# Sigmoid attention, then an MLP mixer: the first two batches mixed singly, and all work written in the order of a model of readiness

One Trainium2 chip (trn2), one core. The metric is the device time of one execution in microseconds (us), lower is better; the output has to agree with the reference.

## The reference

Eight batches, 12 heads, 448 positions, head size 64. Attention with a sigmoid in place of softmax makes x; a mixer with two layers over tokens and two over channels follows.

```python
scores = np.matmul(q, k.transpose(0, 1, 3, 2)) / np.sqrt(64) - np.log(448)
x = np.matmul(1.0 / (1.0 + np.exp(-scores)), v)      # (8, 12, 448, 64)
x = x.transpose(0, 2, 1, 3).reshape(8, 448, 768)
h = np.maximum(x.transpose(0, 2, 1) @ w_tok1, 0.0) @ w_tok2      # 448 -> 256 -> 448
u = x + h.transpose(0, 2, 1)
out = u + np.maximum(u @ w_ch1, 0.0) @ w_ch2                    # 768 -> 1536 -> 768
```

## The kernel before

The batches are taken in four pairs; the two batches of a pair lie on the two halves of the 128 partitions. While TensorE mixes the channels of pair g, the attention of pair g+1 is woven in between. The channel products use Strassen's scheme: seven products in place of eight, paid for by sums of rows of u (the "s" and "r" tiles), sums of weights, and VectorE copies ("c") of partial results. Each engine has a queue of its own and takes it in the order in which the program wrote the instructions, so the written order is part of the design.

The copy that puts one pair of heads into the layout that the transposing DMA takes, on VectorE:

```python
    def permute(g, i, what):
        m = pa.tile([128, J, 2, E], FP16, tag=f"p{what}", bufs=1, name=f"p{what}_{g}_{i}")
        nc.vector.tensor_copy(
            out=m[:, :, :, :], in_=raws[(g, i, what)].rearrange("p h j e -> p j h e")
        )
```

The sums of rows, all on VectorE, and the relu of product 4 of channel layer one, there too:

```python
    def row_sums(a11, a12, a21, a22, s2, s3, s4):
        def one(o, x, y, op):
            return lambda: nc.vector.tensor_tensor(out=o, in0=x, in1=y, op=op)
    # ... (four sums)
            elif p == 4:
                mm(bk[(cb, "x")], 4, cb, False)
                nc.vector.tensor_scalar(
                    out=h[:, cb, :, 1, :],
                    in0=bk[(cb, "x")].rearrange("c (j p) -> c j p", j=J),
                    scalar1=0.0,
                    scalar2=None,
                    op0=MAX,
                )
```

The order: fixed positions, and the attention spread by a cost per piece.

```python
    def weave(mix, side, att, upto):
        each = sum(c for c, _ in mix[:upto]) / (len(att) + 1)
        # ... (before each channel product: as many attention steps as are due)
            f()
            at += c
            # ...
            run(side.get(m, []))
    # ... (for each pair g: sums at fixed places in the list of channel products)
            after(1, lambda g=g: ch1_sums(g, 0, J)[3]())
            # ...
                for j0, j1, ats in (
                    (0, 4, (b1 + 11, b1 + 11, b1 + 12)),
                    (4, 6, (b1 + 14, b1 + 14, b1 + 14)),
                    (6, 7, (b1 + 15, b1 + 15, b1 + 15)),
                ):
```

## Time and profile before

| | before |
|---|---|
| median of the 3 runs made before the change | 437.9 us (433.66 to 438.22) |
| span of the profiled execution | 439.5 us, granted clock 0.957 |
| TensorE busy | 372.5 us, 85% |
| up to the first channel product | 79.4 us |
| the three stages with attention beside the mixing | 95.2, 99.7, 98.6 us |
| last pair's mixing, layer one and layer two | 29.6 and 25.5 us |
| tail without products | 11.6 us |

Stages are cut in TensorE's timeline at the first channel product of each unit. A "gap" is the idle time in brackets that the timeline prints with the first instruction after it, with what released it. A "granted clock" under 1.00 means that the array ran part of the stretch at half clock.

### The profile page before, as it was taken

Reading aid. Unit: us, or ns where it says so; the run is one execution under the profiler, and the core shown is the slowest. Engines: PE = TensorE matmul, PEld = TensorE weight load, DVE = VectorE, ACT = ScalarE, POOL = GpSimd, SP = SyncE. Lnnn points to the kernel's source line nnn. Section 1 sums busy time; section 2 is a strip of 40 time slices with the busy share of each in tenths; the row PEclk is TensorE's granted clock in tenths of the full one; section 3 lists DMA queues with packets and bytes.
Section 4 is the critical chain, followed back from the end, with each engine's and each line's share of the span. In section 5 each row is a group of like instructions: output and inputs, shape, how many; then the busy total and the mean of one; then the engine's idle time right before and its main releaser. Section 6 shows DMA issues by size and latency. Waiting matters only on the chain.

```text
span 439.5 us, 8012 instructions
## 1 busy us (share of the span) xinstructions
PE 372.5 (85%) x3204; PEld 178.6 (41%) x3204; DVE 289.0 (66%) x547; ACT 196.3 (45%) x231; POOL 122.4 (28%) x227
## 2 busy tenths in 40 slices
PE   2888778799799899869979899769999899899990
PEld 1444333344344444324434444324444444344550
DVE  2467656987885488646754578746673578898760
ACT  1897546666366233637656133545776133000000
POOL 8780403033333112243234211332310111000130
PEclk9999969999899999969989999988999999999996
DMA  8999899367556449686677539776670239200232
GB/s 105 192 164 201 120 172 124 50 104 109 84 78 104 102 85 167 119 110 108 98 101 115 108 68 141 148 114 94 104 104 1 73 72 154 81 1 0 72 103 78
DMA packets 74581, 45.39 MB, mean 103 GB/s; under 512 B 51632, under 2 KB 71856, under 8 KB 74544
## 3 DMA queue, kind: packets, MB, share of 16 engines
q0 software_dynamic: 26192, 32.94, 44.4%
q1 hardware_dynamic: 48352, 11.93, 17.4%
q8 instruction: 25, 0.41, 0.4%
q14 instruction: 12, 0.10, 0.1%
HBM read 43.84 MB, written 11.01 MB: 125 GB/s over the span
## 4 chain that ended last, share of the span: by engine, by line
PE 53%; DVE 19%; DMA 11%; ACT 8%; issue 5%; POOL 2%; POOLq 0%; DVEq 0%; ACTq 0%; SPq 0%
PE x L563 8%; PE x L438 7%; PE qk L212 6%; PE xa L228 6%; DMA q<-in_q_dram 6%; ACT attn L219 5%; PE k L295 5%; PE z L563 4%; DVE c L453 4%; PE z L438 4%; PE yn L318 4%; PE d L610 3%; DMA uT<-u 3%; DVE h2T L456 3%; PE xb L255 2%
## 5 line engine op out<-in xcount | busy, mean ns | idle before, releaser
L219 ACT ACTIVATE attn<-qk 128x896 f16<-128x896 f32 x168 | 145.7, 917 | 76.0 <-PE qk L212 69.6
L438 PEld LDWEIGHTS <-w 128*128 128x128 f16 x504 | 46.0, 100 | 78.5 <-issue 47.3
L512 POOL DMA_DIRECT2D out_dram<-u x56 | 29.4, 531 | 149.1 <-DVE u L574 147.1
L212 PE MATMUL qk<-qT,kT 64*64 64x448 f16 x672 | 62.0, 395 | 9.0 <-ACT attn L219 4.9
L453 DVE COPY c<-x 128x448 f32<-128x448 f32 x72 | 44.6, 619 | 15.2 <-PE x L438 13.4
L438 PE MATMUL x<-s,w 128*128 128x448 f16 x144 | 37.2, 369 | 10.4 <-DVE c L453 10.4
L438 PE MATMUL x<-uT,w 128*128 128x448 f16 x144 | 37.4, 371 | 7.8 <-DVE h2T L456 6.0
L228 PE MATMUL xa<-attn,v 64*64 64x448 f16 x672 | 41.3, 366 | 0.0
L202 POOL COPY gate<-qT 1x2 f16<-1x2 f16 x16 | 2.8, 175 | 128.8 <-DMA qT<-pq 128.8
L212 PEld LDWEIGHTS <-kT 64*64 64x64 f16 x672 | 19.5, 109 | 45.5 <-issue 41.3
L574 DVE TENSOR_TENSOR u<-u,x 128x384 f32<-128x384 f32 x48 | 26.5, 551 | 16.5 <-PE x L563 16.0
L107 POOL DMA_DIRECT2D k<-in_k_dram x48 | 29.1, 616 | 25.8 <-DVE pk L161 16.0
L563 PEld LDWEIGHTS <-h2T 128*128 128x128 f16 x288 | 26.3, 98 | 22.4 <-issue 6.8
L327 DVE TENSOR_TENSOR u<-x_nat,yn 128x384 f32<-128x384 f16 x56 | 28.9, 549 | 7.0 <-PE yn L318 6.8
L456 DVE CUSTOM_DVE_ANT_0 h2T<-z,c 128x448 f16<-128x448 f32 x48 | 29.8, 621 | 4.7 <-PE z L438 3.9
L245 ACT ACTIVATE xT<-xa 128x896 f16<-128x896 f32 x18 | 16.5, 917 | 30.6 <-PE xa L228 30.6
L107 POOL DMA_DIRECT2D q<-in_q_dram x48 | 29.2, 626 | 2.4 <-DVE c L453 2.1
L107 POOL DMA_DIRECT2D v<-in_v_dram x48 | 29.4, 638 | 1.0 <-DMA w_tok_t<-in_moe_w_tok_dram 0.6
L346 ACT ACTIVATE u<-u 128x768 f16<-128x768 f32 x21 | 17.7, 843 | 24.6 <-DVE u L327 18.9
L563 PE MATMUL x<-w,r 128*128 128x384 f16 x144 | 27.5, 327 | 0.8 <-DVE u L574 0.8
L574 DVE TENSOR_TENSOR u<-u,z 128x384 f32<-128x384 f32 x24 | 13.2, 552 | 22.5 <-PE z L563 22.3
L318 PE MATMUL yn<-h1T,w_tok_n 128*64 128x384 f16 x224 | 25.4, 339 | 3.1 <-DVE kT L176 1.3
(58 smaller groups left out, 467.2 us busy)
## 6 DMA issues: line engine op xcount, KB each, us to landing
out_dram<-u POOLq DMA_DIRECT2D x56, 192.0 KB, 3.3
k<-in_k_dram POOLq DMA_DIRECT2D x48, 112.0 KB, 2.9
q<-in_q_dram POOLq DMA_DIRECT2D x48, 112.0 KB, 4.1
v<-in_v_dram POOLq DMA_DIRECT2D x48, 112.0 KB, 4.4
w<-in_moe_w_ch_dram POOLq DMA_DIRECT2D x2, 2304.0 KB, 17.6
w_tok_t<-in_moe_w_tok_dram POOLq DMA_DIRECT2D x2, 224.0 KB, 5.8
uT<-u SPq DMA_TRANSPOSE x21, 4.4
kT<-pk SPq DMA_TRANSPOSE x17, 3.3
```

The source lines that it names most:

```text
L107: nc.gpsimd.dma_start(out=t[64 * b : 64 * b + 64, :, :, :], in_=src[2 * g + b, 2 * i : 2 * i + 2].rearrange("h (p j) e -> p h j e", j=J),)
L212: nc.tensor.matmul(out=ps[64 * b : 64 * b + 64, h, 0:S], lhsT=kT[(g, i)][r, j, b, :], rhs=qT[(g, i)][r, :, b, :], start=True, stop=True,)
L219: nc.scalar.activation(out=at[:, :, :], in_=ps[:, :, 0:S], func=SIGMOID, bias=att_bias, scale=att_scale)
L228: nc.tensor.matmul(out=ps[b][64 * h : 64 * h + 64, :], lhsT=vf[r, h, j, :], rhs=attn[(g, i, j)][r, h, :], start=(j == 0), stop=(j == J - 1),)
L318: nc.tensor.matmul(out=ps[64 * b : 64 * b + 64, :], lhsT=w_tok2_n[:, tcb, j, :], rhs=h1T[(g, half, tcb)][:, b, :], start=(tcb == 0), stop= ...
L327: nc.vector.tensor_tensor(out=u_of(g, j)[:, DH * half : DH * half + DH], in0=x_of(g, half)[:, j, :], in1=ps[:, :], op=ADD,)
L438: nc.tensor.matmul(out=ps[:, :], lhsT=W(p, n, cb), rhs=A[p](n), start=(first and n == 0), skip_group_check=True, stop=(n == KD - 1),)
L453: nc.vector.tensor_copy(out=s[:, :], in_=bk[(cb, "x")][:, :])
L456: nc.vector._custom_dve(dve_ops.TENSOR_ADD_SAT, out=h[:, KC * half + cb, :, b, :], in0=ps.rearrange("c (j p) -> c j p", j=J), in1=snap[(cb ...
L512: nc.gpsimd.dma_start(out=out[2 * g + b].rearrange("(p j) d -> p j d", j=J)[:, j, :], in_=us[(g, j)][64 * b : 64 * b + 64, :],)
L563: nc.tensor.matmul(out=ps[:, :], lhsT=A(p, n, kb), rhs=W(p, kb), start=(first and kb == 0), skip_group_check=True, stop=(kb == KC - 1),)
L574: nc.vector.tensor_tensor(out=u, in0=u, in1=ps[:, :], op=ADD)
```

## The change

Its intent: start the channel products sooner by mixing the first two batches (A and B) one at a time, with the two head halves of a single batch on the two partition sides; multiply these directly, without sums or copies; move the rearranging copies and some sums to GpSimd and one relu to ScalarE; and write everything in an order that a small model of costs and readiness gives while the program is built.

```diff
+    UNITS = ["A", "B", 1, 2, 3]
+    SIDES = {
+        "A": ((0, 0), (0, 6)),
+        "B": ((1, 0), (1, 6)),
+        **{g: ((2 * g, 0), (2 * g + 1, 0)) for g in (1, 2, 3)},
+    }
+    BY_DVE = ("A", "B", 1)
+    RELU4 = "act"
+    BANK = 0.4
@@ the copies @@
-        nc.vector.tensor_copy(
+        nc.gpsimd.tensor_copy(
             out=m[:, :, :, :], in_=raws[(g, i, what)].rearrange("p h j e -> p j h e")
         )
+        did("pool", 0.95, [("raw", g, i, what)], [("linear", g, i, what)], 0.1)
@@ the sums of layer two's rows, called r @@
+                nc.gpsimd if n and g < 3 else nc.vector, KC * 128, ("R", g, n), [("h", g)], ...
@@ direct products of a single batch; 72 matmuls here, 168 in layer two @@
+            for n in range(NDB):
+                ...
+                nc.tensor.matmul(
+                    out=ps[:, :],
+                    lhsT=w1[:, n, 128 * cb : 128 * cb + 128],
+                    rhs=uTs[g][:, n % KD, :, n // KD, :],
@@ A's and B's token layer two: fixed banks 2 and 3 of the four @@
+                ops.append(lambda: uturn_single(g, j - 2, 3))
+                ops.append(lambda: tok2_single(g, j, 2))
@@ the model: when is an input there, when is an engine free @@
+    def did(engine, cost, needs, gives, tail=0.0):
+        t = max([clock[engine]] + [there.get(key, 0.0) for key in needs])
+        clock[engine] = t + cost
+        for key in gives:
+            there[key] = t + cost + tail
+        return t
@@ a sum of rows is written when it would be ready for an idle VectorE, or at its last position @@
+                    soon = t_of(keys) <= clock["pe"] and clock["dve"] <= clock["pe"] + 0.2
+                    if soon or pos >= last:
@@ the sums of layer one's rows: last position 1000 products later, that is, none @@
+                    side.append(
+                        (first, first + 1000, keys, lambda g=g, j0=j0, j1=j1, m=m: ch1_sums(g, j0, j1)[m][1]())
+                    )
```

(Cuts: the loads' order, the transposes of the first seven pairs, the lists that `merge` goes through, the rest of `merge`.) The copies of x and the token relu of A, B and pair 1 also go from ScalarE to VectorE (`BY_DVE`).

## The prediction

> **What bounds the kernel now.** I read the page's busy shares first, then the stretches, then single gaps in the timeline and the chain of waits.
>
> ```profile
> PE 372.5 (85%) x3204; PEld 178.6 (41%) x3204; DVE 289.0 (66%) x547; ACT 196.3 (45%) x231; POOL 122.4 (28%) x227
> PE   2888778799799899869979899769999899899990
> ...
> PEclk9999969999899999969989999988999999999996
> ```
>
> TensorE is the busiest engine and works in every slice but the first and the last; no other engine is near full over the span. So the time is TensorE's own work plus its gaps. Where those are, the busy times by stretch show (columns: stretch, length, busy time of PE, PEld, DVE, ACT, POOL with counts, granted clock, DMA share, GB/s):
>
> ```profile
> 0.00:79.40 79.40, 57.81 (x663) 29.02 (x664) 45.44 (x86) 50.10 (x61) 36.90 (x66) 0.94 1.00 153
> 79.40:174.10 94.70, 85.28 (x734) 40.21 (x733) 72.48 (x144) 45.05 (x53) 24.70 (x47) 0.98 0.59 95
> 174.10:273.50 99.40, 89.70 (x767) 41.36 (x766) 62.49 (x116) 50.56 (x59) 28.34 (x54) 0.95 0.69 110
> 273.50:372.90 99.40, 88.85 (x768) 41.26 (x768) 64.02 (x121) 50.63 (x59) 23.78 (x46) 0.97 0.58 96
> 372.90:402.00 29.10, 25.74 (x126) 12.12 (x125) 25.16 (x46) 0.00 (x0) 1.40 (x3) 1.00 0.11 35
> 402.00:428.00 26.00, 25.08 (x153) 14.66 (x150) 18.82 (x37) 0.00 (x0) 6.06 (x12) 1.00 0.25 69
> 428.00:439.50 11.50, 0.00 (x0) 0.00 (x0) 0.54 (x1) 0.00 (x0) 1.25 (x3) 0.71 0.28 86
> ```
>
> Rows: the prologue (attention of batches 0 and 1, no channel product before 79.4 us); three stages, each mixing one pair of batches while the next pair's attention runs beside it; the last pair's mixing in its two layers; the tail, in which only the last stores land. From start-to-start times in TensorE's timeline, a stage of undisturbed work is: 42 score steps of 0.24 us, 10.1; six value products of 1.35, 8.1; six turnings of x of 0.48, 2.9; token products 4 x 1.24 and 7 x 0.77, 10.4; channel layer one, 42 pieces of 0.57, 23.9; layer two, 25 pieces of 0.975, 24.4; about 5 for some fifty changes between whole-array and quarter-array products at 0.1 each. Sum 84.8 us, against 99.4 twice. The missing 14.5 us have a pattern, here in the stage that begins at 174 (TensorE's timeline):
>
> ```profile
> 187.09 0.57 PE L212 MATMUL qk<-qT,kT 64*64 64x448 f16 x8
> 190.68 1.28 PE L438 MATMUL x<-uT,w 128*128 128x448 f16 x3 [3.02 <-DVE h2T L456]
> ...
> 198.66 0.73 PE L438 MATMUL z<-uT,w 128*128 128x448 f16 x3
> ```
>
> And the chain of waits over the same time:
>
> ```profile
> 185.97 3.43 DMA q<-in_q_dram
> 189.40 0.04 DVEq L161
> 189.43 0.04 issue
> 189.48 0.62 DVE pq L161
> 190.10 0.54 DVE h2T L456
> 190.64 0.04 issue
> 190.68 1.28 PE x L438 x3
> ```
>
> VectorE reached the rearranging copy of a q that had not arrived. Behind it in VectorE's queue stood the h2T sum that frees the bank of the next product, so TensorE waited for a load it does not need for another ten microseconds, and came back slow: 1.28 us for three products instead of 0.73, until about 197. The chain shows the same wait at 92 and 103, 218, 285 and 319: two in each of the three stages.
>
> **What the Trainium skill says.** "TensorE: Matmul & The Clock Gate", Part 1: after an idle window of about 3.4 us the array runs at half clock and needs about as long to recover. The trace agrees roughly: after the 3.02 us gap, products run slow for about 6 us; granted clock 0.95 in that stage. The same page, under engine queue depths, calls VectorE's queue strictly first in, first out; the lines above agree. "GPSIMD Engine Reference", 4.1 (engine selection), puts one-input elementwise work on GpSimd near line rate and two-input work about twice as slow as VectorE; GpSimd does no such work in this trace. "SBUF — State Buffer", "Who interferes with whom", says that VectorE instructions with two SBUF inputs and GpSimd instructions that read SBUF exclude each other for a whole instruction; nothing in the trace of before shows it.
>
> **Part 1, the first two batches singly.** The prologue's pace is set by ScalarE's sigmoid, one each 0.87 us (2.60 us for three in a row), after a first at 10.84. Doing batch A alone means 21 before the mixing instead of 42. The first copies fall away, so I take the first sigmoid at 9.4: 9.4 + 21 x 0.87 = 27.7 us. Then, in series: last values 0.5, two copies out 1.3, turning and copy 1.2, token layer one with its relu 3.2, and token layer two, which VectorE paces: per block of rows an add of 0.55 and two short copies of about 0.33 (estimates from 0.60 for twice the width), 7 x 1.21 = 8.5. That gives 42.4. VectorE also serves B's attention then (six turned tiles of 0.62 and copies of x, some 4 us), so channel work begins at about **47 us** instead of 79.4. Loads allow it: one q, k or v costs 1.22 us of issue, so 15 of them, the token weights (2.4 us, an estimate) and w1 (17.6 us to landing) bring w1 at about 40. B's last pair lands behind w1, at about 43, just as B's first 14 score steps end.
>
> **Part 2, direct channel products.** Per single batch: 12 blocks of six 448-wide products at 0.19, 13.7, and 14 half blocks at 0.975, 13.7, together 27.4; two cost 54.8 against 48.3 for the joined stage with its seven products for eight: **6.5 us more** on TensorE. In return there are no sums of rows and no c copies there: VectorE has 24 relu copies in place of 42 copies and sums, so it can't hold up TensorE.
> Work left at 47 until batch pair 1 may be mixed: 54.8, pair 1's attention 35.5 (the 32.2 above without mixing, plus changes), B's rest about 10, changes in A's and B's own products 2: 102. With 6 us of waits: **155** instead of 174.1, 19 saved.
>
> **Part 3, order and engines.** The rearranging copies (48 x 0.61 = 29 us in all, 12 a stage; those of the first seven head pairs vanish into more, smaller TensorE transposes of, I take it, equal total time) leave VectorE for GpSimd, where a late q holds up only GpSimd. The order is chosen so that an instruction is written when its inputs should be there. Each middle stage loses 14.5 us now. About 10 are the two events: roughly 3 us idle and up to 3 us by half clock each, less in the milder ones. I let 5 us remain for bank waits and for what the model of readiness gets wrong: **90 us** per stage, twice 9.4, 19 saved.
> In the last stage, layer one takes 4.49 us per column block (from one block's product to the next in the chain) where seven pieces need 4.0, because VectorE has seven operations per block. The relu of product 4 now goes to ScalarE, idle there: six operations, 3.2 us at their 0.535 pitch, leave slack. Worth 0.45 x 6 = 2.7, and with the sums of the first rows earlier, 3.5: 55.1 becomes **51.5**.
> The tail of 11.5 is one store and the end of the program, untouched.
> Sum: 155 + 90 + 90 + 51.5 + 11.5 = 398, or 399 with a little for GpSimd's sums.
>
> **Rivals.**
> First: GpSimd becomes the holder. Per stage it has 36 load issues of 0.61, 14 stores of 0.53, 12 copies of about 0.95 (896 elements at 0.96 GHz, estimate) and six sums of about 1.85 (estimate at twice VectorE's rate for 768 elements): 22 + 7 + 11 + 11 = 52 of 90 us, so not full, but a queue in order. A store waiting for its u, or a sum that locks VectorE out, may delay a copy and with it a score. For it speak the 147 us it already waits for u; against it that load and scores run several microseconds ahead. Result if so: stages stay near 97, about **414**.
> Second: the gain of the early start is given back. Mixing A starts at 47, but w2 or B's last loads come late, or the token step of B and pair 1 can't keep ahead of a mixing that uses up its work sooner. Gaps above 3 us halve the clock as well. DMA was fully busy (share 1.00) over the whole prologue, which speaks for it; that its demand is the same and the products come later than the loads, against. Result: 155 becomes 166, about **409**.
> Third: the written order is nearly ideal and TensorE runs through: 2 us of waits per stage, 44 us for the first product. That gives about **384**.
>
> **Range and chances.** The middle case is 399; the good rival 384, each bad one 409 to 414, both together about 424. I take 382 to 417. For less than 2% gain (over 429) the stages would have to gain nothing and the start less than half its worth. Faster 0.94, within 2% 0.04, slower 0.02.
>
> **What would show it.** Right: first channel product at 45 to 50 us; no VectorE wait on q or k loads of later pairs; middle stages of 87 to 93 us; TensorE busy about the same in microseconds but near 92% of the span; clock at 0.97 or better in the middle; last layer one near 4.1 us per block. Wrong: a first channel product after 55; GpSimd copies that run late, with score products waiting for kT or qT; VectorE sums much longer than 0.55 while GpSimd works; new gaps of 3 us before channel products.

## The result, and the profile after

| | before | after | predicted |
|---|---|---|---|
| median | 436.42 us of 4 (433.66 to 438.22) | 418.32 us of 4 (415.77 to 419.28) | 399 |
| ratio | 1 | 0.9581 (0.9508 to 0.9655) | |
| first channel product | 79.4 | 66.2 | 47 |
| until pair 1 is mixed | 174.6 | 166.0 | 155 |
| pair 1's mixing | 99.7 | 90.7 | 90 |
| pair 2's mixing | 98.6 | 85.3 | 90 |
| pair 3, layer one + layer two | 29.6 + 25.5 | 34.5 + 27.5 | 51.5 in all |
| tail | 11.6 | 12.5 | 11.5 |
| span | 439.5 | 416.5 | 398 in sum |

A ratio is the mean time of one kernel's fast runs over that of the other's of the same rounds, so not quite the ratio of the medians quoted.

The outputs are right. The change is 4.2% faster; 9% had been predicted. Pair 1's stage came out as predicted and pair 2's 4.7 us shorter. The start and the last pair are each some ten microseconds longer than predicted, and the last pair is even longer than before. First the page of the changed kernel:

```profile
PE 362.4 (87%) x3506; PEld 185.3 (45%) x3506; DVE 249.0 (60%) x444; ACT 182.9 (44%) x221; POOL 182.8 (44%) x287
PE   2878887999999997998979899899999996998960
...
PEclk9999999999999999999999999999999995999995
```

VectorE has 40 us less work and GpSimd 60 more. The clock row has no dips in the middle any more, and a new one at slice 34, where the last pair begins. The same in the busy times by stretch (columns as in the prediction: length, PE, PEld, DVE, ACT, POOL, clock, DMA share, GB/s):

```profile
0.00:66.20 66.20, 47.51 (x707) 26.02 (x708) 31.64 (x55) 41.54 (x49) 35.03 (x61) 1.00 1.03 166
66.20:165.30 99.10, 94.68 (x1021) 50.09 (x1019) 64.70 (x121) 36.67 (x42) 47.24 (x80) 1.00 0.64 112
...
165.30:256.70 91.40, 83.98 (x769) 41.04 (x768) 57.81 (x98) 53.10 (x65) 51.99 (x75) 1.00 0.69 116
256.70:342.00 85.30, 82.19 (x744) 40.27 (x743) 51.24 (x92) 48.38 (x59) 40.15 (x57) 1.00 0.58 104
342.00:376.50 34.50, 29.08 (x128) 13.39 (x127) 24.59 (x43) 3.20 (x6) 1.20 (x3) 0.85 0.09 29
376.50:403.90 27.40, 24.91 (x151) 14.54 (x149) 18.48 (x35) 0.07 (x1) 6.06 (x12) 1.00 0.23 65
403.90:416.50 12.60, 0.09 (x1) 0.00 (x0) 0.55 (x1) 0.00 (x0) 1.14 (x3) 0.61 0.25 78
```

In the middle the granted clock is 1.00 where it was 0.95 and 0.97. In the last pair's layer one it is 0.85, with TensorE at 29.1 busy of 34.5, where before about as many (126 for 128) took 25.7 of 29.1. So layer one lost twice: it waited and it ran slow.

**The wait that is gone.** The groups of copies, before and after (busy us, mean ns; then idle before and its releaser):

```profile
L161 DVE COPY pq<-q 128x896 f16<-128x896 f16 x24 | 14.7, 613 | 14.0 <-DMA q<-in_q_dram 14.0
```

```profile
L248 POOL COPY pq<-q 128x896 f16<-128x896 f16 x17 | 16.0, 939 | 16.6 <-DMA q<-in_q_dram 16.3
```

The wait for a late q still happens, 16.3 us in sum; it stands in GpSimd's queue now, so no sum or copy on VectorE hangs on it. It has not become free: score products wait for a q that is not yet transposed, and the channel products behind them in TensorE's queue wait too. There are four such gaps, 4.4 us in sum, where before it was 0.5; the longest:

```profile
69.10 0.38 PE L321 MATMUL qk<-qT,kT 64*64 64x448 f16 x4 [1.28 <-DMA qT<-pq]
```

The chain of waits behind it runs from a load of q that landed at 65.07 us over GpSimd's copy at 65.19 to the transposing DMA.

**The last pair's opening**, TensorE and VectorE in the timeline of the changed kernel:

```profile
341.98 0.73 PE L555 MATMUL x<-uT,w 128*128 128x448 f16 x3
...
343.17 0.62 DVE L570 COPY c<-x 128x448 f32<-128x448 f32 x1 [0.43 <-PE x L555]
...
344.50 0.35 DVE L474 TENSOR_TENSOR s<-uT 128x384 f16<-128x384 f16 x1
...
345.98 1.27 PE L555 MATMUL x<-s,w 128*128 128x448 f16 x3 [2.70 <-DVE s L474]
...
349.58 2.40 PE L555 MATMUL x<-uT,w 128*128 128x448 f16 x6 [1.20 <-DVE uT L474]
```

Two products need only u and run. The third needs s. The sums that finish s start at 344.50, although the last piece of the turned u had landed at 341.00: the model wrote them after the first copy c and the sum that follows it, and VectorE's queue is in order. TensorE is idle for 2.70 us and comes back at half clock: three matmuls take 1.27 us in place of 0.73, and triples start 1.12 us apart in place of 0.57 until about 355 (the granted clock is 0.50 from 345.4 to 355.5). Before, the same place had gaps of 0.80 and 0.77 and no slow triples.

**A longer sum.** In pair 1's mixing, with GpSimd's sums beside VectorE's:

```profile
211.20 3.29 DVE L474 TENSOR_TENSOR r<-h2T,r 128x768 f16<-128x768 f16 x1
...
214.15 1.84 POOL L474 TENSOR_TENSOR r<-r,h2T 128x768 f16<-128x768 f16 x1
214.42 1.99 DVE L474 TENSOR_TENSOR h2T<-h2T 128x768 f16<-128x768 f16 x1
...
216.92 1.14 PE L759 MATMUL x<-w,h2T 128*128 128x384 f16 x6 [2.71 <-DVE u L771]
```

The VectorE sums take 3.29 and 1.99 us where the two before them took 0.55. Behind them in the queue stands the addition to u that frees a bank, and TensorE waits 2.71 us.

Which sums are stretched can be read from the start and length of every sum and every GpSimd instruction. The 18 VectorE sums of this size that had no GpSimd sum or copy beside them took at most 0.56 us. Four of the six that had one were stretched, to 0.83, 1.21, 1.99 and 3.29 us, and each ended 0.40 to 0.43 us after a GpSimd sum or copy ended; the last lines above show it (215.99 and 216.41). The other two had begun before the GpSimd sum, which then took 2.01 and 2.02 us where seven others took 1.63 to 1.65. VectorE's copies c and its additions to u, which read the bank of a product, kept their 0.62 and 0.55 us beside GpSimd. The first 1.2 us of the 3.29 lie beside load issues of GpSimd and are not explained by this.

**The start.** TensorE between the last scores of A and its channel products:

```profile
37.34 2.45 PE L381 MATMUL k_A<-x_nat_A,w_tok_t 64*128 64x384 f16 x28 [0.43 <-ACT attn_B L328]
...
41.36 0.52 PE L409 MATMUL yn_A<-h1T_A,w_tok_n 128*64 128x384 f16 x4
...
46.63 0.52 PE L409 MATMUL yn_A<-h1T_A,w_tok_n 128*64 128x384 f16 x4
```

The seven token blocks of A run from 41.4 to 62.9, one to five microseconds apart, with B's score steps between them, many of these after a gap of about 0.4 us for ScalarE's sigmoid. ScalarE itself was busy for 24.5 of the 37.2 us from 29.0 to 66.2.

### The profile page after: what moved, and what is told of

Same layout as the page of the kernel before. It is cut to its first block, busy times and chain, and to the rows that moved or that the text cites. A ratio compares the mean times of both kernels' runs of the same rounds, so it can differ in the third digit from the quotient of the medians.

```text
span 416.5 us, 8524 instructions
## 1 busy us (share of the span) xinstructions
PE 362.4 (87%) x3506; PEld 185.3 (45%) x3506; DVE 249.0 (60%) x444; ACT 182.9 (44%) x221; POOL 182.8 (44%) x287
## 4 chain that ended last, share of the span: by engine, by line
PE 60%; DVE 14%; DMA 11%; POOL 4%; ACT 4%; issue 4%; POOLq 0%; DVEq 0%; SPq 0%; ACTq 0%
PE x L759 8%; PE x L555 7%; DMA q<-in_q_dram 6%; PE xa L339 5%; PE qk L321 4%; PE z L759 4%; PE z L555 4%; PE k L381 4%; PE c_B L649 4%; PE yn L409 3%; PE c_A L649 3%; DMA qT<-pq 3%; PE c_A L677 3%; DVE r L474 2%; ACT attn_A L328 2%
## 5 line engine op out<-in xcount | busy, mean ns | idle before, releaser
L328 ACT ACTIVATE attn<-qk 128x896 f16<-128x896 f32 x126 | 110.2, 915 | 96.6 <-PE qk L321 96.4
L555 PEld LDWEIGHTS <-w 128*128 128x128 f16 x378 | 35.8, 100 | 49.5 <-issue 23.5
L570 DVE COPY c<-x 128x448 f32<-128x448 f32 x54 | 33.6, 621 | 28.1 <-PE x L555 27.6
L321 PE MATMUL qk<-qT,kT 64*64 64x448 f16 x504 | 39.4, 361 | 5.5 <-DMA qT<-pq 4.4
L759 PEld LDWEIGHTS <-h2T 128*128 128x128 f16 x216 | 19.7, 98 | 23.3 <-issue 11.6
L691 POOL DMA_DIRECT2D out_dram<-u x28 | 15.2, 560 | 30.8 <-DVE u L689 30.8
L339 PE MATMUL xa<-attn,v 64*64 64x448 f16 x504 | 27.3, 352 | 0.2 <-ACT attn L328 0.2
L555 PE MATMUL z<-s,w 128*128 128x448 f16 x108 | 25.4, 361 | 0.0
L248 POOL COPY pq<-q 128x896 f16<-128x896 f16 x17 | 16.0, 939 | 16.6 <-DMA q<-in_q_dram 16.3
L328 ACT ACTIVATE attn_A<-qk_A 128x896 f16<-128x896 f32 x21 | 17.5, 931 | 11.2 <-PE qk_A L321 11.2
L248 POOL COPY pk<-k 128x896 f16<-128x896 f16 x17 | 16.5, 972 | 11.7 <-DMA k<-in_k_dram 8.7
L759 PEld LDWEIGHTS <-r 128*128 128x128 f16 x162 | 14.9, 98 | 15.2 <-issue 5.1
```

The lines of the kernel that those rows point to most:

```text
L248: nc.gpsimd.tensor_copy(out=m[:, :, :, :], in_=raws[(g, i, what)].rearrange("p h j e -> p j h e"))
L321: nc.tensor.matmul(out=ps[64 * b : 64 * b + 64, h, 0:S], lhsT=kT[(g, i)][r, j, b, :], rhs=qT[(g, i)][r, :, b, :], start=True, stop=True,)
L328: nc.scalar.activation(out=at[:, :, :], in_=ps[:, :, 0:S], func=SIGMOID, bias=att_bias, scale=att_scale)
L339: nc.tensor.matmul(out=ps[b][64 * h : 64 * h + 64, :], lhsT=vf[r, h, j, :], rhs=attn[(g, i, j)][r, h, :], start=(j == 0), stop=(j == J - 1),)
L555: nc.tensor.matmul(out=ps[:, :], lhsT=W(p, n, cb), rhs=A[p](n), start=(first and n == 0), skip_group_check=True, stop=(n == KD - 1),)
L570: nc.vector.tensor_copy(out=s[:, :], in_=bk[(cb, "x")][:, :])
```

## The experiments

All are edits of the changed kernel; ratios are to the kernel before, in the same rounds. The changed kernel has 0.9581 in its first rounds and 0.9542 when run again. "B's end" is the end of B's last channel product, 165.3 in the changed kernel; pair 1's stage counted from there is 91.4.

### 1. The last pair's row sums written earlier

```diff
-                        (first, first + 1000, keys, lambda g=g, j0=j0, ...
+                    last = first + 1000 if g < 3 else base[g] - {0: 2, 4: 1, 6: 0}[j0]
+                        (first, last, keys, lambda g=g, j0=j0, ...
-            for m, key in ((2, "S2"), (3, "S1")):
+            for m, key in ((2, "S2"), (3, "S1")) if g < 3 else ((3, "S1"), (2, "S2")):
+                last = first + 1000 if g < 3 else base[g] + {3: 2, 2: 6}[m]
```

> Only the last pair's row sums are written earlier (those of row blocks 0 to 5 before the last products of the stage before, the last one before the first copy, the third sum before the fourth). Theory A (the last stage lost its gain because these sums stand in VectorE's queue behind the first copy and the first h2T sum, and the two gaps of 2.70 and 1.20 us then put TensorE at half clock until about 355): the first ten microseconds of the last stage have no gap above 1 us and no half clock, the stage from its first product to the last is 54 to 56 us instead of 61.9, and the time falls by 6 to 8 us, ratio to the changed kernel about 0.983. Theory B (the turned u of the last row blocks lands late, so the sums can't start earlier whatever the order): VectorE now waits for the transfer with everything behind it, the gap stays, and the time moves by less than 2 us.

Measured: 412.03 us (411.01 to 414.74), ratio 0.9416 (0.9353 to 0.9478). Layer one of the last pair takes 28.9 us in place of 34.5, the whole last stage 56.4 in place of 62.0. Its opening in the timeline:

```profile
342.09 0.73 PE L555 MATMUL x<-uT,w 128*128 128x448 f16 x3
...
344.13 0.73 PE L555 MATMUL x<-s,w 128*128 128x448 f16 x3 [0.74 <-DVE c L570]
...
346.22 1.11 PE L555 MATMUL x<-uT,w 128*128 128x448 f16 x5 [0.79 <-DVE c L570]
```

No long gap, no half clock. So the place of these sums in VectorE's queue explains 5.6 us of the last stage directly, and the time moved by about as much (6.3 us between the medians). The rival, a turned u that lands too late for earlier sums, is out: its last piece landed at 341.67 us here, and the sums that finish s ran from 341.40 to 343.54.

### 2. A's token layer in two other banks

```diff
+            yb, ub = (0, 1) if g == "A" else (2, 3)
-                ops.append(lambda: uturn_single(g, j - 2, 3))
+                ops.append(lambda: uturn_single(g, j - 2, ub))
-                ops.append(lambda: tok2_single(g, j, 2))
+                ops.append(lambda: tok2_single(g, j, yb))
```

> Batch A's token layer two and the turning of its u use the two banks m0 and m1, free then, in place of m2 and m3, which B's turned tiles and turned x use at the same time; the written order follows from it. Theory A (the start of the mixing at 66 us instead of my 47 is due to A's seven token blocks being strung out from 41 to 66 us by these banks and by B's score steps): A's first channel product comes at 56 to 60 us, the pieces of A fill the gaps between B's score steps, B's last channel product ends at 158 to 162 instead of 165.3, and the time falls by 3 to 7 us. Theory B (ScalarE's sigmoids and the pair banks of the scores set the pace up to there, and TensorE only does the same work in another order): the first product moves, the end of B's channel products stays within 1.5 us of 165.3, and so does the time.

Measured: 421.76 us (418.6 to 425.74), ratio 0.9607; the profiled execution was slow, so its stages are read with care. The first channel product comes at 57.7, 8.5 us sooner; B's end comes at 168.5. TensorE is idle 8.5 us after 57.7, with single gaps of 1.74 behind a copy of xT and 2.54 behind a transposed q. The fast runs, 0.9607 against 0.9581, show no gain: the early start is given back. The start moved as theory A said, B's end did not.

### 3. The rearranging copies on VectorE again

```diff
-        nc.gpsimd.tensor_copy(
+        nc.vector.tensor_copy(
```

The written order is unchanged, as the model still books the copy on GpSimd.

> The rearranging copies of the 17 later head pairs go back to VectorE; every engine's order is otherwise the same. Theory A (moving these copies off VectorE's queue is what shortened the middle stages from 99.4 to 91 and 85 us): the two middle stages are 94 to 100 us, with gaps above 2 us before channel products that end with an h2T sum or copy behind a copy of q, half clock after them, and the time rises by 8 to 18 us. Theory B (the written order alone did it, since a copy is now written only when its load should be there): the stages stay within 3 us and the time rises by under 4 us.

Measured: 429.03 us (426.29 to 430.92), ratio 0.9792. B's end is at 169.5, the middle stages take 94.6 and 89.3. VectorE's group of copies of q, and one of TensorE's two longest gaps after the start (the other, 2.87 us at 274.97, also ends a chain that began with a late q on VectorE):

```profile
L248 DVE COPY pq<-q 128x896 f16<-128x896 f16 x17 | 10.4, 613 | 6.3 <-DMA q<-in_q_dram 5.6 <-issue 0.7
```

```profile
177.44 1.28 PE L555 MATMUL x<-uT,w 128*128 128x448 f16 x3 [2.70 <-DVE c L570]
```

The waits for q on VectorE are back, but at 5.6 us for 17 copies in place of 14.0 for 24 (those for k at 3.7 in place of 10.3): in the new order more of the copies stand where the loads have landed. Taking the copies off VectorE is worth 9 to 11 us in all, about 4 of it in each middle stage and 4 before B's end. The rest of the middle stages' gain, some 14 of 22 us, belongs to the rest of the change, of which the order is one part.

### 4. All row sums on VectorE

```diff
-                engine.tensor_tensor(out=o, in0=x, in1=y, op=op)
+                nc.vector.tensor_tensor(out=o, in0=x, in1=y, op=op)
```

> The twelve row sums that GpSimd makes in the two middle stages (and, with them, no others) go to VectorE at the same places of the order. Theory A (GpSimd's sums locked VectorE's two-input sums: one took 3.29 us, another 1.99 instead of 0.55, and TensorE stood 2.71 us at 216.9): no VectorE sum over 1 us is left in the stages, that gap falls below 1 us, the first middle stage is 2 to 3 us shorter and the time falls by 1 to 3 us. Theory B (the load on VectorE counts more): the sums for blocks one and two delay its adds by as much, and the time stays within 1.5 us or rises.

Measured: 413.68 us (412.53 to 414.43), ratio 0.9444. The middle stages take 89.5 (from B's end) and 84.6; the gap of 2.71 is gone. The group of in-place sums in the changed kernel, and in this one:

```profile
L474 DVE TENSOR_TENSOR h2T<-h2T 128x768 f16<-128x768 f16 x9 | 6.4, 713 | 4.7 <-POOL r L474 4.7
```

```profile
L474 DVE TENSOR_TENSOR h2T<-h2T 128x768 f16<-128x768 f16 x9 | 5.0, 550 | 0.0
```

VectorE does twelve sums more, about 6.6 us of work at 0.55 each, and the kernel is faster: GpSimd's help cost more than it gave. Two VectorE sums still take 1.42 and 2.47 us, beside GpSimd's copies; each ends about 0.42 us after such a copy, so not only sums on GpSimd stretch them. One or two microseconds of the total lie in the last pair's layer one (32.3 for 34.5), which this edit does not touch: there the half clock ended sooner in this execution.

### 5. The relu of product 4 on VectorE again

```diff
-                relu(RELU4, h[0][:, cb, :, 1, :], ...)
+                relu("dve", h[0][:, cb, :, 1, :], ...)
```

> The relu of product 4 of layer one goes back from ScalarE to VectorE in all three pairs' mixing; every engine's order is otherwise the same. Theory A (VectorE's seven operations per column block held layer one of the last pair at 4.49 us a block, and giving one away brought it to 4.33): the blocks of the last stage take 4.5 to 4.9 us again, that stage is 1 to 3 us longer, and the time rises by 1 to 5 us with the two middle stages. Theory B (what paces a block is the chain from a product over its copy c to the next product, 4.33 us with or without the relu): the last stage stays within 0.5 us and the time within 1.5 us.

Measured: 415.44 us (414.45 to 418.1), ratio 0.9515, against 0.9542 for the changed kernel on the same chip: the same. From one column block to the next of the last layer one it takes 4.49 us again, as before; in the changed kernel it is 4.33 (359.11, 363.44, 367.78, 372.11). So the relu's move is worth 0.16 us a block, about 1 us in all.

### The changed kernel again, for the runs of the same chip

> The changed kernel itself, unedited, on the chip of the three others, so that they can be set against it in the same rounds: 0.955 to 0.962 of the kernel before, some 418 to 421 us.

Measured: 416.89 us (416.43 to 417.38), ratio 0.9542 (0.9465 to 0.9618); first channel product 66.1, B's end 165.4, stages 91.4 and 85.0, last layer one 33.0. The picture is stable, but for 1.5 us of half clock in the last layer one. One difference teaches something of the clock. The gap before the first products of layer two is here too, a little shorter:

```profile
215.36 1.79 PE L759 MATMUL x<-w,h2T 128*128 128x384 f16 x6 [2.55 <-DVE u L771]
```

Six matmuls take 1.79 us, and the granted clock is 0.50 from 215.7 to 219.1. In the first execution the gap of 2.71 us at the same place was followed by 1.14 us for the six and a clock of 1.00. So the same gap of the same kernel may or may not bring half clock.

### 6. No slack for banks in the model

```diff
-    BANK = 0.4
+    BANK = 0.0
```

One constant of the model. A bank that will be free in 0.4 us no longer counts as free, so the written order is another; not one instruction changes its engine.

> The model's slack of 0.4 us, by which a second score step may be written before its bank is free, is set to zero; all that follows from it is a different order. Theory A (TensorE's idle 7.7 us between 29 and 66 us is mostly some fifteen waits of 0.3 to 0.5 us for ScalarE before a score step, work written too early by that slack, and is part of the 10 us by which batches A and B ended later than I predicted): that idle falls to 3 to 5 us, B's last product ends at 161 to 163.5 instead of 165.3 and the time falls by 1 to 4 us. Theory B (there is no other ready work to put into those waits, since B's attention is at ScalarE's pace and A's token steps depend on each other): the end of B's products stays within 1 us or comes later, and the time does not fall.

Measured: 432.35 us (431.63 to 434.3), ratio 0.9899. The first channel product comes at 64.5 and B's end at 165.7, but the middle stages take 100.2 and 90.8. In pair 1's stage:

```profile
262.74 2.83 PE L339 MATMUL xa<-attn,v 64*64 64x448 f16 x28 [4.27 <-ACT attn L328]
```

A value product was written just behind the scores that it needs, and TensorE waited 4.27 us for ScalarE. With the engines all as in the change, this order gives back 3.6 of the 4.6% that the changed kernel gained in the same rounds. Of the two theories, the one that saw nothing to gain was right.

### 7. The best of these in one: early sums, row sums on VectorE, sums of the last layer two spread

```diff
+                    lo, hi = first, first + 4 if n == 0 else first + 7
+                    if g == 3:
+                        st = {0: 0, 1: 1, 3: 2, 2: 3}[m]
+                        lo = {0: c2 + 2 + st, 1: c2 + 5 + st, 2: b1 + 1 + st}[n]
+                        hi = lo
+                    side.append((lo, hi, [("h", g)] + done, block_sum(n, m)))
```

In the changed kernel the four sums of a block of layer two are written together, and two gaps of 0.95 and 1.28 us stand behind them in the last pair. Here one sum goes between two products.

> Three edits together: the last pair's row sums early (first experiment), the middle stages' GpSimd row sums on VectorE (fourth), and in the last stage's layer two the row sums of the blocks of rows written one at a time between VectorE's adds in place of four in a row. If they add up: about 6.5 from the first, 2 from the second (most of what that run gained beyond it lay in the half-clock time of the last stage, which the first edit removes too), and about 2 from the third, since the waits of 0.95 and 1.28 us before products of layer two go away: 408 to 411 us, ratio to the kernel before 0.93 to 0.94. If the third edit only moves the waits, 410 to 413.

Measured: 405.99 and 408.4 us in the fast runs, 413.77 and 415.74 in two that were slow; ratio 0.9317 (0.9212 to 0.9421). The last pair by stretches:

```profile
337.00:365.70 28.70, 25.37 (x128) 12.27 (x126) 23.65 (x42) 3.14 (x6) 1.29 (x3) 1.00 0.11 35
365.70:391.70 26.00, 25.05 (x152) 14.48 (x149) 17.84 (x35) 0.13 (x1) 6.18 (x12) 1.00 0.24 69
```

54.7 us for the last pair, where the kernel before took 55.1 and the prediction said 51.5.

### 8 to 10. Earlier starts

Three ways to bring A's or B's channel products forward: run 8 has run 2's banks and loads pair 1's second head pair ahead of w2; run 9 gives B's first two value products the banks m0 and m1; run 10 has both that load order and those banks, on top of run 7.

```diff
@@ runs 8 and 10 @@
+        load_pair(1, 1)
         nc.gpsimd.dma_start(
             out=w2[:, :, :], in_=moe_w_ch2.rearrange("(cb c) d -> c cb d", cb=NCB)
         )
         did("load", 12.6, [], ["w2"], 2.0)
-        load_pair(1, 1)
@@ runs 9 and 10 @@
+        if g == "B" and i < 2:
+            pb = [bank(f"xa_{g}_{i}_{b}", [128, S], at=b) for b in range(2)]
```

> As the second experiment (A's token layer in banks m0 and m1), and the heads of the second head pair of batches 2 and 3 are loaded before w2, not behind it: in the second experiment the earlier start at 57.7 us was followed by waits for qT (2.54 us at 120) and other gaps, 8.5 us idle in all to the end of B. Theory A (the late head loads took the gain of the earlier start away): those waits for qT between 58 and 165 us sum to under 1 us, B's last product ends at 160 to 163, and the time falls by 2 to 5 us below the changed kernel. Theory B (up to B's end TensorE has about 125 us of work from 29 us on, whatever starts first, and an earlier start of A only leaves less to do beside attention later): B's end stays at 164 to 168 and the time within 2 us.

> The value products of B's first two head pairs go to banks m0 and m1, idle at that time, in place of a pair bank of the scores, which each takes out of the scores' turn for some 3 us. Theory A (score steps and value products that share two pair banks make TensorE and ScalarE wait for each other between 29 and 66 us: 7.7 us of TensorE's idle time and 12.7 of ScalarE's in 37.2): the idle time of TensorE from 29 us to A's first product falls to under 5 us, B's attention is done some 3 us earlier, B's last product ends at 161 to 163.5 and the time falls by 2 to 4 us. Theory B (as in the second and sixth run, what is gained before A's first product is lost again by B's end): B's end within 1.5 us of 165.3, the time within 1.5 us.

> The three edits of the seventh experiment together with the value banks of the ninth and the load order of the eighth. If the gains before B's end hold, 2 to 5 us below the seventh, 402 to 408 us (0.922 to 0.933 of the kernel before); if not, the same as the seventh, whose fast runs were 406 and 408 us.

| run | median us | ratio | first channel product | B's end |
|---|---|---|---|---|
| changed kernel | 418.32 | 0.9581 | 66.2 | 165.3 |
| 8 | 430.65 | 0.9867 | 57.7 | 174.8 |
| 9 | 424.3 | 0.9689 | 63.3 | 176.4 |
| 10 | 421.52 | 0.9634 | 59.1 | 179.5 |

All three start sooner and end later. In run 8:

```profile
75.57 0.59 PE L321 MATMUL qk<-qT,kT 64*64 64x448 f16 x4 [5.76 <-DMA qT<-pq]
```

A score product whose q was not yet transposed stood in TensorE's queue ahead of A's products. Run 9 waits 2.78 us for B's k, whose load lies behind w1, and then in smaller pieces. That raised the question whether the weights' loads set B's end.

### 11 to 13. No weight loads (a wrong result)

Three kernels without the two loads of w1 and w2: VectorE fills both with zeros at the start, so the result is wrong, while every product, sum and copy is the same. Run 11 is the changed kernel, run 12 has run 9's banks, run 13 run 2's.

```diff
-        nc.gpsimd.dma_start(
-            out=w1[:, :, :], in_=moe_w_ch1.rearrange("(db d) c -> d db c", db=NDB)
-        )
@@ and the same for w2 @@
+        nc.vector.memset(w1[:, :, :], 0.0)
+        nc.vector.memset(w2[:, :, :], 0.0)
```

> Wrong result on purpose: w1 and w2 are set to zero by VectorE at the start and not loaded, 9.4 MB less from memory; every engine's order is otherwise that of the changed kernel. Theory A (the transfers that stand behind w1 and w2 set how soon batches A and B can be done): the waits for qT near 69 us go, B's last product ends at 161 us or earlier instead of 165.3. Theory B (in this order the loads are in time, and TensorE's 125 us of work after 29 us plus its waits for ScalarE and VectorE set the end): B's end stays at 164 to 166 us.

> Wrong result on purpose: the ninth experiment (B's values in banks of their own) without the weight loads. There B ended at 176.4 us, after waits of 2.78 us for k of B's third pair (at 44 us, behind w1) and 1.45 for qT. Theory A (an earlier start failed because the loads were not there): without the weight loads B ends at 158 to 163 us. Theory B (it failed because the changed order leaves other waits: for ScalarE, for VectorE's copies): B still ends at 170 or later.

> Wrong result on purpose: the second experiment (A's token layer in banks m0 and m1, first product at 57.7 us, B's end at 168.5) without the weight loads. Theory A (loads): the wait of 2.54 us for qT goes and B ends at 159 to 164. Theory B (the order): B ends at 166 or later.

| run | median us | ratio | first channel product | B's end | gaps over 1 us between the first score and B's end |
|---|---|---|---|---|---|
| 11 | 416.03 | 0.9494 | 69.8 | 166.8 | 1.15, 1.04 |
| 12 | 421.66 | 0.9622 | 61.2 | 171.7 | 2.26, 1.13, 1.46 |
| 13 | 422.39 | 0.9639 | 60.6 | 171.5 | 1.74, 2.25, 1.33, 1.85 |

The filling with zeros delays the first score from 9.06 to 11.54 us, so run 11's B's end is at about 164.3 when that is taken off: 1 us from the changed kernel. Its stretch from A's first channel product to B's end:

```profile
69.80:166.80 97.00, 94.57 (x1019) 49.93 (x1023) 65.11 (x122) 36.56 (x42) 42.78 (x72) 1.00 0.58 107
```

94.6 us of TensorE's work in 97.0, against 94.7 in 99.1 with the loads. The loads cost the changed kernel at most about the 2 us of this difference. Run 12 ends B 4.7 us before run 9, and some 7 us before it when the same delay is taken off; run 9 had lost 11.1 to the changed kernel. There the loads were the larger part, and about 4 us are waits and slower products of the order. Run 13 ends B about where run 2 did (171.5, or 169.0 without the delay, against 168.5). So the theory that the weights' loads set B's end is refuted for the changed order and for run 2's, not for run 9's.

### 14. The best version again, five rounds

The edit is that of run 7.

> The seventh experiment's kernel once more with more rounds: 406 to 409 us in most runs, and up to 416 in some, as before; ratio 0.925 to 0.94.

Measured: 410.32 us (406.89 to 418.85, six runs, one of them slow), ratio 0.9357 (0.9299 to 0.9415). Last pair 28.7 and 26.0, stages 88.8 and 84.0, B's end 168.0. The best version is about 2% faster than the change, and 6.4% faster than the kernel before. Its trace ends B 4.7 us later than that of run 7, the same kernel. One wait stands out:

```profile
70.33 0.38 PE L321 MATMUL qk<-qT,kT 64*64 64x448 f16 x4 [1.80 <-DMA qT<-pq]
```

The q of this score landed at 66.32 us here and at 63.34 in run 7, which has no gap there. After the gap the granted clock is 0.50 from 70.7 to 74.1; in run 7 it is 1.00.

## Why the prediction was wrong in size

**Right: the direction and, in sum, the two middle stages.** 90.7 and 85.3 against 90 each (87 to 93 was named): 22 us saved where 19 were forecast. The named cause, VectorE waiting for q and k at the head of its queue, was real: 24.3 us of such waits are gone, and so is the half clock in the middle (0.95 and 0.97 to 1.00). But the credit is shared with the order: moving the copies back (run 3) costs 9 to 11 us, about 8 of them in these stages, and a worse order with the copies on GpSimd (run 6) 14 to 15; the two are not a sum, as each acts through the other. So there was luck in how well the figure for these stages fits. And more than half of the gain was not idle time: in the two stages together TensorE's idle time, added up from its timeline, fell from 19.0 to 10.3 us, and the time in which it was occupied, with nearly the same products, from 179.3 to 165.7. About 8 of these 13.6 us are the half clock (0.05 and 0.03 of 99.4 us each).

**The first rival happened, in a small form.** "A sum that locks VectorE out" cost one gap of 2.71 us in pair 1's stage. Run 4 cured it by giving all sums back to VectorE. The lock that the prediction quoted, and that nothing in the trace of before showed, fits the trace of after: 3.29 and 1.99 us in place of 0.55, each ending just after a GpSimd instruction, and nothing over 0.56 without one beside it. A late q also delayed scores, by 4.4 us in sum; at the longest of these waits the load was late, not GpSimd's copy. The prediction's 1.85 us for a GpSimd sum does not follow from its stated basis, as twice VectorE's 0.55 is 1.1; that 1.63 to 2.02 was measured is luck. Of the signs of being wrong that it named, three came: a first channel product after 55, VectorE sums much longer than 0.55, and scores that wait for qT.

**Failed step one: the last pair, "with the sums of the first rows earlier, 3.5: 55.1 becomes 51.5".** It became 62.0. I had read in the diff that sums are written as soon as they are ready, and took that for earlier. In fact the condition also asks for an idle VectorE by the model's clock, and the last position was put 1000 products away, so the sums slipped behind other work. The order of before had fixed places at the end of the pair before. Run 1 restores those: 5.6 us. The second term, "worth 0.45 x 6 = 2.7" for the relu, measured 0.16 x 6, about 1 (run 5): the pitch fell from 4.49 to 4.33 only, though VectorE had one operation less. And the clumped sums of layer two, of which I had not thought, made it 27.5 for 25.5; spread, they give 26.0 (run 7). With both orders mended the last pair takes 54.7, 0.4 us less than before. No run came nearer to 51.5.

**Failed step two: "work left at 47 ... 102. With 6 us of waits: 155".** Pair 1's mixing began at 166.0 and B's end was at 165.3. The striking miss is the first channel product at 66 rather than 47. The step that failed there is the chain "in series" for A: its last sigmoid ended at 30.8 us where 27.7 was predicted, its token layer one began at 37.3 where the sum gives 30.7, and its token layer two, put at 7 x 1.21 = 8.5 us, ran from 41.4 to 62.9. The banks that it shares with B's turned tiles account for 8.5 us of the late start, as run 2 shows. But the late marker by itself isn't what cost the time: TensorE did other work meanwhile, and five orders with a start sooner by 2 to 9 us (runs 2, 6, 8, 9 and 10) have B's end between 165.7 and 179.5, none before 165.3. The sum from TensorE's own timeline, from 47 to B's end, shows which terms were wrong (time from start to start less idle):

| term | predicted | measured |
|---|---|---|
| A's and B's direct channel products | 54.8 | 58.4 |
| pair 1's attention and token step | 35.5 | 33.0 |
| what was left of B | 10 | 13.0 |
| what was left of A's token step | 0 | 4.6 |
| changes between shapes in A's and B's own products | 2 | in the first row |
| seven score steps of pair 2, done ahead | 0 | 1.9 |
| waits | 6 | 7.4 |
| sum | 108 | 118.3 |

The direct products, the changes and pair 1 together came to 91.4 us where 92.3 had been predicted (the prediction's "32.2 above" for pair 1 is a slip: its parts add up to 31.5). The rest is that at 47 the kernel was not where I had put it: 9.5 us more of A's, B's and pair 2's work lay between there and B's end. A's chain was to run through in series while B's steps filled the gaps, and in the written order its steps alternate with B's. TensorE was idle 4.6 us between 29 and 47, and 3.1 from there to 66.2. My second rival had named 166, the figure that came, but by coincidence: one of its causes, that the weights come late, is refuted by run 11 for this order, and the other, a mixing that runs out of work, fits ill with waits of 7.4 us where 6 were allowed, which is an argument and not a test.

**Open.** Whether any order removes these 7.7 us is not settled: of the ways to do it that were tried, each bought its earlier start with longer waits and slower products later. Also open is what spreads the best version's ten runs from 406 to 419 us; there is no clear step between those called fast and slow (run 14 has fast ones at 410.84 and 412.95). The granted clock falls with the time, from 0.989 to 0.975 in run 7's four runs. The two traces show one such place, the late q at 70 us with half clock after it; both are of fast runs, so the slowest ones stay unexplained.

## What to carry to other kernels

Where an engine's queue is in order, a copy that waits for a transfer belongs on the engine whose queue holds up the least (here TensorE still waited 4.4 us for q); but an engine beside which the busy one's sums took up to 3.29 us in place of 0.55 is no free helper for sums. When a model writes the order, give the few operations that open the next stage a latest position: "when ready and idle" let them slip, and here that cost 5.6 us, part of it waiting and part half clock after the wait. And an earlier start marker is no gain by itself; count occupied and idle time of the bounding engine up to the point where the next stage must begin.

## What the Trainium skill lacked or had wrong

- "TensorE: Matmul & The Clock Gate", Part 1, gives an idle window of about 3.4 us before half clock and about as long to recover. In the changed kernel a gap of 2.70 us was enough (345.98, triples at 1.27 us), and the slow phase lasted about 10 us with a second gap of 1.20 in it. A gap of 2.71 us at 216.92 was followed by full speed (six matmuls of 384 columns in 1.14), and one of 2.55 at the same place in the next run of the same kernel by half clock (1.79). In the kernel before, a gap of 2.07 us at 225.01 was enough (clock 0.50 from 224.6 to 227.9). The page's remark that the window runs freely fits such a difference; its figure as a safe limit for a gap doesn't (the same Part tells of half clock after frequent short idle spells, without their length).
- "GPSIMD Engine Reference", sections 3.1 and 4.1, puts two-input work at about twice VectorE's time, measured on fp32. For fp16 sums of 768 elements a partition GpSimd took 1.63 to 2.02 us and VectorE 0.55: about three times (the 2.01 and 2.02 stood behind sums of VectorE). The page calls one-input work roughly line rate without a time for fp16: a copy of 896 fp16 elements took GpSimd 0.94 to 0.97 us on average, VectorE 0.61.
- "TensorEngine Tiling (Array Packing)", "Key Properties", says that changing the tiling drains the array, without a time. Estimated from this trace: the direct channel products took 58.4 us in 42 stretches between other work, where 54.8 was worked out for them undisturbed, so at most about 0.09 us a stretch; that the drain is all of it is not shown.
